# Attention and FFN in one kernel: the scores' second pass on half of TensorE's rows, a fifth PSUM bank, W_out sums on another engine, and a new order

## The chip, the cores and the metric

The kernel runs on one core of a Trainium2 chip. A core has TensorE (PE in the profile, with its weight loads listed as PEld), VectorE (DVE), ScalarE (ACT), GpSimd (POOL) and SyncE (SP, which issues the DMAs here). Each engine works through its own queue in the order in which it was filled, and waits on semaphores for the others. The metric is the device time of one execution in microseconds (us); what is compared is the median of several runs.

## The reference

Block-causal attention over 8 batches, 8 heads, 576 positions and a head size of 64, followed by a feed-forward block. All arithmetic is fp32.

```python
scores = q @ k.T / sqrt(64)                    # per batch and head, 576 x 576
scores = where(block_i >= block_j, scores, -1e9)   # blocks of 64 positions
attn = softmax(scores)
x = (attn @ v) -> (4608 tokens, 512)
h = x @ w_in                                   # 512 x 2048
g = h * sigmoid(h)
out = g @ w_out                                # 2048 x 512
```

## The kernel before

**fp32 by two halves.** TensorE's fast form for fp32 data ("fp32r" in the code) keeps fewer bits of each number, so most products are made of a rounded part ("hi") and what is left ("lo"). For the scores, a unit's tile `qk` holds the transposed q and k of one head twice, in partitions 0 to 63 and again in 64 to 127. `split_hi` (ScalarE) rounds it into `qh`. `split_k` (GpSimd) replaces the k part in partitions 64 to 127 with the remainder, so that a matmul with all 128 rows adds up k_hi and k_lo in one go. `split_q` (GpSimd) makes `ql`, the remainder of q. The scores are then two passes over the same keys: k times `qh`, and k times `ql`.

**Units.** A unit is one head of one batch (u0 to u63); it handles the 448 query positions from 128 on. (The first 128 positions are done ahead of that, by the objects a, b and c0 to c3.) The keys are cut into five groups of at most 128 (`SEG`): group 0 with 448 queries, group 1 with 448, group 2 with 320, group 3 with 192 and group 4 (64 keys) with 64. `scores` makes ten matmuls for a unit: pass one and pass two of key group 0, then of groups 2, 3, 1 and 4. Their results lie in three PSUM banks (`BANKS`): group 0 in the first, groups 2 and 3 in the second, groups 1 and 4 in the third. Units take the three banks in turn from four (`NS = 4`, S0 to S3). VectorE then takes maxima (`max`), subtracts them (`sub`), ScalarE takes the exponentials (`exp`), GpSimd and VectorE sum them, and for every second unit `pv` multiplies the exponentials of two units with v, in plain fp32, on two halves of TensorE's columns (tile `U`).

**The FFN.** The products x times w_in (`ffn1`, tokens `ffn` in the order; tile `h`) use the same hi and lo parts, three products of the four. One `ffn` token is half of a tile of h, six matmuls with 448 tokens each in the batches after the first positions; there are 320 of them. `keep` copies h out of PSUM and `save` writes it to DRAM. The second product (`prod`, at the end) is a Strassen-like scheme that needs sums of quarters of w_out and of g. The sums of w_out are made by the objects t0 to t7: `Turned.x` makes three sums, `hi` rounds, `lo` makes the remainder; `bits` of the objects o0 to o15 ahead of it rebuild w_out's numbers from the words in which they arrive, by way of the PSUM bank SC.

**What sets the order.** `ORDER` is a long string of tokens, worked through from left to right; each token calls one method and so appends its instructions to the engines' queues. `u20.scores` calls `Unit.scores` of unit 20; `ffn` calls the next half of h; `warm:10` issues ten small matmuls that no result uses. Nothing else moves instructions. Tiles and PSUM banks are handed out in that order too, and the waits between engines follow from it.

**The lines.** L702 is the matmul of the scores, L805 that of `pv`, L1031 that of the FFN's first product, L1108 that of the second. L834 is `warm`. L906, L934, L972 and L1003 are small matmuls for the first positions, on quarters (64 rows by 64 columns) or halves of TensorE. L683 is `split_k`, L687 `split_q`, L616 to L620 are the sums of w_out, L635 its remainders, and L541 the first step of `bits`.

Of the kernel before, what the change touches and what calls it, by code (L numbers as in the profile page):

```python
# [68 lines left out]
a.load b.load a.load_v w0.load b.load_v warm:10 a.scores w1.load w2.load a.max:0 a.sub:0 warm:3 b.scores c0.load a.max:1 a.sub:1  # L69
b.max:0 a.exp w3.load b.max:1 w4.load a.sum w0.rebias w0.sign w5.load b.sub:0 w6.load a.norm b.sub:1 w7.load w0.bits:0 b.exp  # L70
w0.bits:2 o1.load w1.rebias w1.sign warm:30 a.turn:0 b.sum w0.hi a.turn:1 a.back:0 w8.load w0.lo a.back:1 w1.bits:0 w2.rebias
warm:2 a.pv o0.load w1.bits:2 b.norm a.hi:0 c0.load_v a.hi:1 a.lo:0 w1.hi a.lo:1 w2.sign warm:7 b.turn:0 w3.rebias c3.load
c0.scores:0 b.back:0 b.turn:1 w5.rebias w1.lo w2.bits:0 w4.rebias ffn c0.max:0 b.back:1 w3.sign w2.bits:2 c0.exp:0 w9.load b.pv
w3.bits:0 c0.scores:1 w10.load all.mask b.hi:0 w3.bits:2 b.hi:1 ffn w2.hi c0.max:1 c3.load_v w3.hi w2.lo b.lo:0 c0.exp:1 b.lo:1
w4.bits:0 w3.lo ffn c0.sum w6.rebias c1.load w4.bits:1 w7.rebias c0.norm w4.bits:2 ffn keep w11.load w8.rebias w5.bits:0 w4.hi
save c0.turn:0 w5.bits:1 keep w4.lo c3.scores:0 w12.load c0.back:0 w5.bits:2 o1.rebias c0.turn:1 c3.max:0 w5.hi ffn save w6.bits:0
c0.back:1 w5.lo c3.exp:0 w6.bits:1 w13.load c0.pv w6.bits:2 c3.scores:1 c0.hi c1.load_v w7.bits:0 w6.hi ffn c0.lo w10.rebias
w14.load w6.lo c3.max:1 w9.rebias w7.bits:1 c3.exp:1 c1.scores:0 w7.bits:2 ffn c1.max:0 w15.load keep c3.sum c1.exp:0 save
w8.bits:0 c3.norm ffn w8.bits:1 w7.hi w8.bits:2 c1.scores:1 keep w7.lo w9.bits:0 c3.turn:0 w11.rebias save c1.max:1 w8.hi c2.load
ffn w9.bits:1 c3.back:0 w8.lo c1.exp:1 w9.bits:2 c3.turn:1 ffn w10.bits:0 c3.back:1 c1.sum w10.bits:1 w9.hi c1.norm c3.pv keep  # L80
w10.bits:2 w12.rebias ffn save w11.bits:0 w10.hi w9.lo w13.rebias w11.bits:1 c1.turn:0 o0.rebias w11.bits:2 ffn w10.lo c1.back:0
w12.bits:0 w11.hi w14.rebias c1.turn:1 w12.bits:1 w11.lo ffn c1.back:1 w12.bits:2 keep w13.bits:0 w15.rebias save c1.pv w12.hi
w13.bits:1 ffn w12.lo c1.hi c2.load_v w13.bits:2 c1.lo w13.hi c2.scores:0 w14.bits:0 keep w13.lo w14.bits:1 save ffn u0.load
c2.max:0 w14.bits:2 c2.exp:0 ffn w15.bits:0 w15.bits:1 w14.hi c2.scores:1 w15.bits:2 keep w14.lo ffn save c2.max:1 w15.hi u1.load
o0.bits:0 w15.lo all.staged c2.exp:1 ffn o0.bits:1 o0.bits:2 u0.split_hi ffn c2.sum o2.load o1.bits:0 c2.norm keep o1.bits:1
t0.hi:0 ffn save o1.bits:2 u0.split_q t0.hi:1 o3.load c2.turn:0 keep ffn u0.split_k c2.back:0 save c2.turn:1 ffn u2.load t0.x:0
c2.back:1 t0.x:1 c2.pv t0.hi:2 keep t0.x:2 u0.load_v ffn c2.hi save t0.lo:0 c3.hi u2.load_v c2.lo t0.hi:3 u3.load_v t0.lo:2 ffn
c3.lo u1.load_v t0.lo:3 u0.scores keep u0.max:0 t0.lo:1 save u0.max:1 ffn u1.split_hi u0.max:2 o2.rebias ffn u1.split_q u0.gather
o2.bits:0 o3.rebias u1.split_k u0.top ffn o2.bits:1 u0.spread u0.wide keep u3.load ffn u0.sub:0 u0.sub:1 save u0.exp:0 u1.scores
u0.sub:2 u0.exp:1 u0.exp:2 u1.max:0 ffn u1.max:1 u2.split_hi u0.add:0 u1.max:2 keep ffn u2.split_q u0.sums:0 u1.gather save  # L90
o2.bits:2 u0.add:1 u1.top ffn u1.spread o4.load o3.bits:0 u2.split_k u1.wide keep t1.hi:0 ffn u0.sums:1 save u1.sub:0 u4.load
t1.lo:0 u1.sub:1 u1.exp:0 u2.scores keep u1.sub:2 u1.exp:1 save u2.max:0 ffn u1.exp:2 u2.max:1 u3.split_hi u1.add:0 u2.max:2 u1.pv
u3.split_q u1.sums:0 u2.gather o3.bits:1 u2.top u3.split_k o3.bits:2 u2.spread ffn o5.load t1.hi:1 u2.wide u5.load u1.add:1
u2.sub:0 u2.sub:1 u3.scores t1.x:0 u2.exp:0 u4.load_v keep u3.max:0 u5.load_v u2.exp:1 save u1.sums:1 t1.x:1 ffn u4.split_hi
u3.max:1 t1.x:2 u3.max:2 t1.hi:2 ffn u4.split_q t1.hi:3 u2.sub:2 u3.gather u4.split_k ffn u1.sums_x u2.exp:2 u3.top u2.sums:0
u3.spread ffn u6.load u1.sums_g u2.add:0 u3.wide keep u3.sub:0 u2.add:1 u3.sub:1 save u4.scores u3.exp:0 keep u4.max:0 u1.sums_m
u3.exp:1 u2.sums:1 save ffn u5.split_hi u3.sub:2 u4.max:1 u5.split_q u3.exp:2 ffn u4.max:2 u3.add:0 ffn u1.inverse keep u4.gather
u1.mult save u3.add:1 u3.pv u4.top u3.sums:0 u4.spread u5.split_k u3.sums:1 u1.x_hi u4.wide u3.sums_x u4.sub:0 u7.load u1.x_lo
u3.sums_g u4.sub:1 u5.scores u4.exp:0 u6.load_v u4.sub:2 u3.sums_m u4.exp:1 u7.load_v u5.max:0 u4.exp:2 ffn u5.max:1 u6.split_hi
u4.add:0 u5.max:2 ffn keep u3.inverse u6.split_q u5.gather save ffn u5.top u3.mult u5.spread u4.add:1 u4.sums:0 u3.x_hi u5.wide  # L100
u6.split_k ffn keep u4.sums:1 save u5.sub:0 ffn u5.sub:1 u8.load u3.x_lo u5.exp:0 u5.sub:2 u5.exp:1 t1.lo:3 u6.scores u5.exp:2
u6.max:0 keep u5.add:0 u6.max:1 u5.pv save u7.split_hi u6.max:2 u5.add:1 u5.sums:0 u6.gather u7.split_q u5.sums:1 u6.top ffn
u5.sums_x u8.load_v u6.spread u7.split_k u9.load_v u5.sums_g u6.wide ffn u6.sub:0 u9.load u5.sums_m u6.sub:1 u6.exp:0 u7.scores
u6.sub:2 u6.exp:1 u6.exp:2 u7.max:0 t1.lo:1 u7.max:1 ffn keep u8.split_hi save u7.max:2 u6.add:0 ffn o5.rebias u5.inverse
u8.split_q u7.gather u5.mult ffn keep u7.top u6.add:1 u6.sums:0 u7.spread save u8.split_k ffn u5.x_hi u7.wide o4.rebias u6.sums:1
u7.sub:0 ffn u10.load u5.x_lo keep u7.sub:1 u7.exp:0 save u7.sub:2 u7.exp:1 t1.lo:2 u8.scores o4.bits:0 u7.exp:2 u8.max:0 u7.add:0
u7.pv u8.max:1 u9.split_hi u8.max:2 u7.add:1 u9.split_q u7.sums:0 u8.gather u7.sums:1 ffn u10.load_v u8.top u7.sums_x u9.split_k
u8.spread o4.bits:1 u11.load_v u7.sums_g u8.wide ffn u8.sub:0 keep u11.load u7.sums_m u8.sub:1 u8.exp:0 u9.scores save u8.sub:2
u8.exp:1 u9.max:0 u8.exp:2 ffn u9.max:1 u10.split_hi u8.add:0 u9.max:2 ffn u10.split_q keep u7.inverse u9.gather save u10.split_k
ffn u9.top u7.mult u9.spread u8.sums:0 u7.x_hi u9.wide ffn u12.load u7.x_lo keep u9.sub:0 u9.sub:1 save u9.exp:0 u8.add:1  # L110
u10.scores u9.sub:2 u9.exp:1 u10.max:0 u9.exp:2 u9.pv u10.max:1 u11.split_hi u10.max:2 u11.split_q u8.sums:1 u10.gather u9.sums:0
ffn u11.split_k u12.load_v u10.top o4.bits:2 u10.spread u13.load_v u10.wide t2.hi:0 ffn u13.load u9.add:0 keep u10.sub:0 u10.sub:1
u10.exp:0 save u9.add:1 u11.scores u10.sub:2 u10.exp:1 t2.lo:0 u11.max:0 u10.exp:2 ffn u9.sums:1 u12.split_hi u11.max:1 u10.add:0
ffn u11.max:2 keep u12.split_q save u9.sums_x u11.gather u10.sums:0 ffn u11.top u10.add:1 u9.sums_g o5.bits:0 u11.spread
u12.split_k ffn u10.sums:1 keep u11.wide u11.sub:0 save ffn u9.sums_m u14.load u11.sub:1 u11.exp:0 u12.scores u11.sub:2 u11.exp:1
u11.exp:2 u12.max:0 u12.max:1 ffn keep u11.add:0 u13.split_hi save u12.max:2 ffn u11.add:1 u9.inverse u12.gather u13.split_q ffn
# [1132 lines left out]
```

## Time and profile before

The columns of the last four rows are us of busy time of each engine in a stretch of the span.

| | |
|---|---|
| median of 3 runs | 999.03 us (998.24 to 1000.21) |
| the profiled execution | 999.48 us, of which the span of the program is 997.8 us |
| 0 to 76 us: first positions, weights | PE 71.53, DVE 53.85, ACT 55.14, POOL 47.28 |
| 76 to 560 us: the 64 units, with FFN between | PE 484.00, DVE 431.60, ACT 356.00, POOL 381.08 |
| 560 to 628 us: the rest of the first product; w_out is prepared | PE 68.00, DVE 28.70, ACT 38.92, POOL 43.03 |
| 628 to 998 us: the second product | PE 363.65, DVE 254.23, ACT 242.28, POOL 144.63 |

A matmul's end in the profile is modelled and matmuls overlap in it, so PE's busy time does not tell whether TensorE was at its peak. The distance from one matmul's start to the next tells it better: in the rows of the timeline the first column is the start, the second how long the row lasts.

### The profile page before, as it was taken

To read this page: it belongs to the slowest core of one execution; us is meant where nothing else is said; L and a number is where in the kernel's file an instruction comes from. 1 tells how busy PE (TensorE), PEld (TensorE's weight loads), DVE (VectorE), ACT (ScalarE), POOL (GpSimd) and SP (SyncE) were. 2 spreads that over 40 slices of the span, in tenths; PEclk is the share of its full clock that TensorE was granted. 3 is DMA by queue.
4 is the path that set the end of the run, shared out by engine and by line. 5 is a ranking of instruction groups with operands and counts; after the bars stand their busy time and mean duration, and the time that the engine had idled before them with its cause. 6 is when DMAs were issued, how large, how long until landed. Compare 5 with 4: busy or idle time off the path is not lost. (4 is left out here: it accounts for less than half of the span.)

```text
span 997.8 us, 20716 instructions
## 1 busy us (share of the span) xinstructions
PE 987.2 (99%) x6936; PEld 888.9 (89%) x6936; DVE 768.4 (77%) x1969; ACT 692.4 (69%) x1555; POOL 616.0 (62%) x722
## 2 busy tenths in 40 slices
...
GB/s 351 387 195 187 170 144 154 151 145 149 159 147 147 149 159 142 146 166 144 145 149 148 76 208 216 179 164 154 127 128 132 145 128 127 128 126 143 135 43 44
DMA packets 109803, 155.51 MB, mean 156 GB/s; under 512 B 18560, under 2 KB 83072, under 8 KB 109696
## 3 DMA queue, kind: packets, MB, share of 16 engines
...
## 5 line engine op out<-in xcount | busy, mean ns | idle before, releaser
L1031 PE MATMUL h<-x,wi 128*128 128x448 f32 (+2 forms) x1968 | 422.4, 370 | 0.3 <-POOL wi L563 0.3
L1031 PEld LDWEIGHTS h<-x,wi 128*128 128x128 f32 x1968 | 357.3, 188 | 37.4 <-issue 0.9
L642 DVE TRANSPOSE_TENSOR_REDUCE Mx<-S 64x4 f32<-64x128 f32 (+4 forms) x384 | 130.4, 399 | 18.1 <-PE S L702 17.1
L755 ACT ACTIVATE p<-T 128x512 f32<-128x512 f32 (+1 forms) x192 | 114.2, 613 | 21.0 <-DVE T L745 16.1
L1037 ACT COPY g<-h 128x448 f32<-128x448 f32 (+1 forms) x160 | 86.4, 540 | 50.9 <-PE h L1031 36.0
L1096 POOL TENSOR_TENSOR x<-raw,x 128x512 fp32r<-128x512 f32 (+1 forms) x58 | 58.8, 1016 | 78.2 <-ACT x L1092 73.9
L1059 ACT ACTIVATE raw<-raw 128x1024 f32<-128x1024 f32 x72 | 76.3, 1061 | 41.7 <-DMA raw<-gdb 36.4
L1096 POOL TENSOR_TENSOR wi<-raw,wi 128x512 fp32r<-128x512 f32 (+1 forms) x56 | 56.7, 1017 | 77.6 <-ACT wi L1092 67.5
L761 POOL TENSOR_TENSOR pa<-p 128x448 f32<-128x448 f32 x64 | 73.5, 1149 | 48.4 <-ACT p L755 41.2
L683 POOL TENSOR_TENSOR qh<-qk,qh 64x576 fp32r<-64x576 f32 x64 | 91.4, 1428 | 5.0
L702 PE MATMUL S<-qh 128*128 128x448 f32 (+3 forms) x320 | 92.8, 303 | 0.0
L687 POOL TENSOR_TENSOR ql<-qk,qh 128x448 fp32r<-128x448 f32 x64 | 73.6, 1149 | 24.0 <-ACT qh L677 17.0
L677 ACT CAST qh<-qk 128x1024 fp32r<-128x1024 f32 x64 | 67.1, 1048 | 28.8 <-PE S L702 15.1
L805 PE MATMUL U<-p,v 128*64 128x448 f32 (+3 forms) x640 | 86.5, 416 | 0.0
L702 PE MATMUL S<-ql,qh 128*128 128x448 f32 (+3 forms) x320 | 83.9, 306 | 0.0
L805 PEld LDWEIGHTS U<-p,v 128*64 128x64 f32 x640 | 43.0, 137 | 42.3 <-issue 31.0
L748 DVE TENSOR_TENSOR T<-S,MR 128x384 f32<-128x384 f32 (+2 forms) x192 | 73.3, 408 | 0.0
L702 PEld LDWEIGHTS S<-ql,qh 128*128 128x128 f32 (+1 forms) x320 | 57.0, 178 | 6.5
L702 PEld LDWEIGHTS S<-qh 128*128 128x128 f32 (+1 forms) x320 | 56.8, 178 | 3.7
L764 POOL TENSOR_TENSOR pa<-pa,p 128x320 f32<-128x320 f32 x64 | 55.9, 873 | 2.5
L1096 POOL TENSOR_TENSOR gc<-raw,gc 128x512 fp32r<-128x512 f32 (+1 forms) x30 | 30.4, 1017 | 41.4 <-ACT gc L1092 33.5
L727 ACT COPY m<-m 32x14 f32<-32x14 f32 x192 | 38.7, 202 | 20.1 <-DVE m L723 18.0
...
## 6 DMA issues: line engine op xcount, KB each, us to landing
qk<-in_qk_dram SPq DMA_DIRECT2D x128, 256.0 KB, 3.8
gdb<-g SPq DMA_DIRECT2D x128, 224.0 KB, 2.3
...
```

Source lines behind the costliest of these rows:

```text
L642: nc.vector.tensor_reduce(out=out, in_=in_, axis=AX.X, op=op, apply_transpose=True)
L683: nc.gpsimd.tensor_tensor(out=u.qh[r, c], in0=u.raw[r, c], in1=u.qh[r, c], op=ALU.subtract)
L687: nc.gpsimd.tensor_tensor(out=u.ql, in0=u.raw[:, :NQ], in1=u.qh[:, :NQ], op=ALU.subtract)
L702: nc.tensor.matmul(u.ps(c, w, m), u.kk[r, j * P : j * P + m], q[r, q0 : q0 + w], start=qq == 0 and not (ROWS and seg in (2, 4)), stop=qq = ...
L748: nc.vector.tensor_tensor(out=u.T[:, c + 64 : c + w], in0=u.ps(c + 64, w - 64), in1=u.mb[:, q0 + 64 : q0 + w], op=ALU.subtract)
L755: nc.scalar.activation(u.p[:, c:e], u.T[:, c:e], AF.Exp, scale=SCALE)
L761: nc.gpsimd.tensor_tensor(out=u.pa, in0=u.p[:, :NQ], in1=u.p[:, 960 : 960 + NQ], op=ALU.add)
L805: nc.tensor.matmul(U[64 * e : 64 * e + 64, q0 : q0 + w], u.vv[:, e, j], z.p[:, c : c + w], start=n == 0, stop=n == 4)
L1031: nc.tensor.matmul(o, wi[wt][:, c, w], x_of(g, c, xt), start=c + k == 0, stop=c == CT - 1 and k == 2)
L1037: nc.scalar.copy(g, hs.pop(z)[:, :n])
L1059: nc.scalar.activation(u.raw, u.raw, AF.Silu)
L1096: e.tensor_tensor(out=u.goal(1, k), in0=u.source(k), in1=u.goal(0, k), op=ALU.subtract)
```

## The change

- `ROWS = True`: the second pass (with `ql`) of key groups 0, 2 and 3 uses 64 rows of TensorE in place of 128. Group 0 uses partitions 0 to 63 and groups 2 and 3 use partitions 64 to 127. The product k_lo times q_lo is left out for these groups. Groups 1 and 4 keep all 128 rows.
- For that, the halves of k are laid otherwise (`LOWS`): keys 0 to 255 have their remainder in partitions 64 to 127 as before, keys 256 to 575 in partitions 0 to 63. `split_k` is two instructions in place of one.
- The passes come in another order (`PASSES`): first pass of groups 0, 2, 3; second pass of 0, 2, 3; then groups 1 and 4 as before.
- `NS = 5`: a unit's three banks are taken in turn from five; the bank SC is the fifth. `bits` for w_out works in its own tile instead of SC.
- `X_BY_VECTOR = (0,)` and `LO_BY_VECTOR = (1, 3)`: for t3 to t7 the first of the three sums and two of the four remainders are made by VectorE in place of GpSimd.
- A new `ORDER`, with the same tokens but for `warm` (63 small matmuls in place of 52).

```diff
-NS = 4
...
-LO_BY_VECTOR = ()
+LO_BY_VECTOR = (1, 3)
+X_BY_VECTOR = (0,)
+NS = 5
...
-ROWS = False
+ROWS = True
...
 if ROWS:
-    LOWS = [(64, 0, 128), (64, 384, 576), (0, 128, 384)]
-    PASSES = [(i, 0, (0, 128)) for i in range(5)] + [(4, 1, (0, 64)), (1, 1, (64, 128)), (0, 1, (0, 64)), (3, 1, (64, 128)), (2, 1, (0, 64))]
+    LOWS = [(64, 0, 256), (0, 256, 576)]
+    FULL, LOW, HIGH = (0, 128), (0, 64), (64, 128)
+    PASSES = [(0, 0, FULL), (1, 0, FULL), (2, 0, FULL), (0, 1, LOW), (1, 1, HIGH), (2, 1, HIGH), (3, 0, FULL), (3, 1, FULL), (4, 0, FULL), (4, 1, FULL)]
 else:
     LOWS = [(64, 0, 576)]
     PASSES = [(i, k, (0, 128)) for i in range(5) for k in range(2)]
...
             elif j == 0:
-                u.a = bank("C").bitcast(U32)
+                u.a = (bank("C") if u.kind == "in" or NS < 5 else u.w).bitcast(U32)
...
         def x(u, k):
 
             q, sub = u.w, ALU.subtract
+            e = nc.vector if u.d >= NTA and k in X_BY_VECTOR else nc.gpsimd
             if k == 0:
                 u.sums = sp.tile([P, 4, 256], F32, tag="xs", name="xs")
-                nc.gpsimd.tensor_tensor(out=u.sums[:, 0:2], in0=q[:, 1:4:2], in1=q[:, 0:2], op=sub)
+                e.tensor_tensor(out=u.sums[:, 0:2], in0=q[:, 1:4:2], in1=q[:, 0:2], op=sub)
...
         def lo(u, k):
             s, n = u.source(k)
-            e = nc.vector if k in LO_BY_VECTOR else nc.gpsimd
+            e = nc.vector if u.d >= NTA and k in LO_BY_VECTOR else nc.gpsimd
...
         def scores(u):
-            banks = [bank((3 * u.i + k) % NS) for k in range(3)]
+            banks = [bank((0, 1, 2, 3, "C")[(3 * u.i + k) % NS]) for k in range(3)]
...
-                nc.tensor.matmul(u.ps(c, w, m), u.kk[r, j * P : j * P + m], q[r, q0 : q0 + w], start=qq == 0 and not (ROWS and seg in (2, 4)), stop=qq == 1, skip_group_check=ROWS)
+                nc.tensor.matmul(u.ps(c, w, m), u.kk[r, j * P : j * P + m], q[r, q0 : q0 + w], start=qq == 0 and not (ROWS and seg == 2), stop=qq == 1 and not (ROWS and seg == 1), skip_group_check=ROWS)
```

(In `PASSES` the first number is a place in `SEG`: 0 is key group 0, 1 is group 2, 2 is group 3, 3 is group 1, 4 is group 4.)

**TensorE, the scores of unit 40.** A row is: line, instruction, output tile, inputs, and the output's shape (partitions by columns, so 64x64 is key group 4). `qh` alone on the right is pass one, `ql,qh` is pass two. Before, from the first score to key group 1:

```order
L702 MATMUL S_5337<-qh 128x448
L702 MATMUL S_5337<-ql,qh 128x448
L702 MATMUL S_5338<-qh 128x320
L702 MATMUL S_5338<-ql,qh 128x320
L702 MATMUL S_5338<-qh 128x192
L702 MATMUL S_5338<-ql,qh 128x192
L702 MATMUL S_5339<-qh 128x448
```

Now (three lines were added above, so L702 is L705):

```order
L705 MATMUL S_5436<-qh 128x448
L705 MATMUL S_5437<-qh 128x320
L705 MATMUL S_5437<-qh 128x192
L705 MATMUL S_5436<-ql,qh 128x448
L705 MATMUL S_5437<-ql,qh 128x320
L705 MATMUL S_5437<-ql,qh 128x192
L705 MATMUL S_5438<-qh 128x448
```

The three `ql,qh` rows now stand together, and these three are the ones on 64 rows; the rows ahead of and behind them use all 128.

**TensorE, the product with v that follows unit 40's scores (L805, now L808, for units 38 and 39).** Before:

```order
L702 MATMUL S_5339<-qh 64x64
L702 MATMUL S_5339<-ql,qh 64x64
L805 MATMUL U<-p,v 64x448 x4
L805 MATMUL U<-p,v 64x320 x2
L805 MATMUL U<-p,v 64x192 x2
L805 MATMUL U<-p,v 64x64 x2
L1031 MATMUL h<-x,wi_78 128x448 x2
```

Now:

```order
L705 MATMUL S_5438<-qh 64x64
L705 MATMUL S_5438<-ql,qh 64x64
L1034 MATMUL h<-x,wi_78 128x448 x2
L1034 MATMUL h<-x,wi_79 128x448
L1034 MATMUL h<-x,wi_78 128x448 x2
L1034 MATMUL h<-x,wi_79 128x448
L808 MATMUL U<-p,v 64x448 x4
L808 MATMUL U<-p,v 64x320 x2
```

One half of h (six matmuls) now stands between the scores and the product with v. Of the 32 such products, 25 stood right behind a unit's scores and 8 do now.

**GpSimd, in the middle of the units.** Before:

```order
L761 TENSOR_TENSOR pa<-p 128x448
L687 TENSOR_TENSOR ql<-qk,qh 128x448
L764 TENSOR_TENSOR pa<-pa,p 128x320
L683 TENSOR_TENSOR qh<-qk,qh 64x576
L817 TENSOR_TENSOR x<-xu,x 128x448
```

Now:

```order
L764 TENSOR_TENSOR pa<-p 128x448
L690 TENSOR_TENSOR ql<-qk,qh 128x448
L767 TENSOR_TENSOR pa<-pa,p 128x320
L686 TENSOR_TENSOR qh<-qk,qh 64x256
L686 TENSOR_TENSOR qh<-qk,qh 64x320
L820 TENSOR_TENSOR x<-xu,x 128x448
```

The remainder of k is two instructions of 256 and 320 columns in place of one of 576.

More of the change, by code (lines that the diff above doesn't have):

```diff
@@ L68 @@
 ORDER = """
[L69 to L116, printed above, removed]
@@ L384 @@
[L384 to L386 removed]
+a.load b.load_v b.load a.load_v w0.load warm:10 a.scores w1.load w2.load a.max:0 c0.load a.max:1 a.sub:0 a.sub:1 warm:10 b.scores
+w3.load a.exp a.sum w4.load w5.load w6.load b.max:0 a.norm w0.rebias b.max:1 w7.load b.sub:0 b.sub:1 w1.rebias w0.sign warm:19
@@ new lines @@
+c0.sum b.hi:1 c3.load_v all.mask b.lo:0 w4.hi b.lo:1 ffn c0.norm keep w5.rebias save w6.rebias c3.scores:0 w5.bits:0 w7.rebias
+w4.lo c0.turn:0 w5.bits:1 w12.load w8.rebias c3.max:0 ffn c0.back:0 w5.bits:2 c3.exp:0 w6.bits:0 w13.load c0.turn:1 ffn w6.bits:1
+c0.back:1 keep w6.bits:2 c0.pv w5.hi save w7.bits:0 w6.hi w14.load w5.lo c3.scores:1 c0.hi w7.bits:1 c1.load_v w9.rebias ffn c0.lo
+w6.lo w10.rebias c3.max:1 o1.rebias w7.bits:2 c1.scores:0 c3.exp:1 o1.bits:0 w15.load ffn w8.bits:0 c1.max:0 keep c3.sum c1.exp:0
@@ new lines @@
+save ffn w8.bits:1 c3.norm o1.bits:1 w8.bits:2 ffn w7.hi o1.bits:2 keep w7.lo w9.bits:0 w8.hi save c3.turn:0 w11.rebias o3.load
+w9.bits:1 c1.scores:1 w8.lo c3.back:0 ffn w9.bits:2 w12.rebias c2.load c1.max:1 w9.hi w10.bits:0 c1.exp:1 w9.lo c3.turn:1
+w10.bits:1 ffn w10.bits:2 c3.back:1 c1.sum ffn keep w11.bits:0 c1.norm w10.hi save w11.bits:1 o0.rebias c3.pv keep w11.bits:2
+w14.rebias w10.lo save o0.bits:0 c1.turn:0 w11.hi ffn w12.bits:0 c1.back:0 w11.lo o0.bits:1 w13.rebias w12.bits:1 c1.turn:1
@@ new lines @@
+w15.rebias ffn o0.bits:2 c1.back:1 w12.bits:2 t0.x:0 o2.load c1.pv w13.bits:0 w12.hi keep w12.lo w13.bits:1 ffn c1.hi save
+w13.bits:2 c2.load_v t0.x:1 c1.lo w13.hi ffn t0.x:2 w14.bits:0 w13.lo w14.bits:1 c2.scores:0 keep w14.bits:2 ffn save c2.max:0
+w14.hi u0.load w15.bits:0 c2.exp:0 w14.lo ffn w15.bits:1 w15.bits:2 c2.scores:1 keep ffn w15.hi save c2.max:1 u1.load w15.lo
+all.staged c2.exp:1 ffn u0.split_hi c2.sum ffn c2.norm keep t0.hi:0 ffn save t0.hi:1 t0.hi:2 u0.split_q t0.hi:3 c2.turn:0 keep ffn
@@ new lines @@
+u5.load_v u2.wide ffn keep o4.bits:1 u5.load u1.sums_m u2.sub:0 u3.scores u2.sub:2 save u2.exp:0 u2.sub:1 u2.exp:2 t1.lo:2 ffn
+u4.split_hi u3.max:0 u3.max:1 u2.add:0 u2.exp:1 ffn u3.max:2 keep u4.split_q save u2.sums:0 u3.gather ffn u1.inverse u2.add:1
+u3.top u1.mult u3.spread ffn u4.split_k u2.sums:1 keep u3.wide u1.x_hi save ffn o4.bits:2 u6.load u1.x_lo u3.sub:0 t2.hi:0
+u3.sub:2 u3.exp:0 u4.scores t2.lo:0 keep u3.sub:1 u3.exp:2 t1.lo:3 save ffn u4.max:0 u3.exp:1 u4.max:1 u5.split_hi u3.add:0
@@ new lines @@
+u27.max:1 u28.split_hi ffn u27.max:2 u26.add:1 keep u28.split_q u26.sums:0 save ffn u27.gather u26.sums:1 u27.top u25.inverse
+u28.split_k u27.spread ffn keep u27.wide u25.mult save ffn u30.load u27.sub:0 u25.x_hi u27.sub:2 u27.exp:0 u28.scores u25.x_lo
+keep u27.sub:1 u27.exp:2 save ffn u28.max:0 u27.exp:1 u27.add:0 u28.max:1 u29.split_hi u27.pv u28.max:2 u27.add:1 u27.sums:0
+u29.split_q u28.gather u27.sums:1 u28.top u27.sums_x u28.spread u29.split_k ffn u30.load_v u27.sums_g u28.wide u31.load_v
@@ new lines @@
+u34.add:0 u35.max:2 ffn u36.split_q u34.sums:0 u35.gather ffn u33.inverse keep u34.add:1 u35.top u33.mult save u35.spread ffn
+u36.split_k u34.sums:1 u33.x_hi u35.wide ffn keep u35.sub:0 u38.load u33.x_lo u35.sub:2 u35.exp:0 u36.scores u35.sub:1 save
+u35.exp:2 u36.max:0 u35.add:0 u35.exp:1 u35.pv u36.max:1 u37.split_hi u36.max:2 u35.add:1 u37.split_q u35.sums:0 u36.gather
+u35.sums:1 ffn u38.load_v u36.top u35.sums_x u39.load_v u37.split_k u36.spread ffn keep u36.wide u35.sums_g save u36.sub:0
```

566 lines of the change are left out of this document (294 added, 272 removed).

## The prediction

> **What bounds the kernel now.** I read the page first, then busy time by stage, then who waited for whom, and last the timeline of one unit.
>
> ```profile
> PE 987.2 (99%) x6936; PEld 888.9 (89%) x6936; DVE 768.4 (77%) x1969; ACT 692.4 (69%) x1555; POOL 616.0 (62%) x722
> 0.00:76.00 76.00, 71.53 (x832) 59.38 (x833) 53.85 (x89) 55.14 (x146) 47.28 (x50) 1.00 0.88 312
> 76.00:560.00 484.00, 484.00 (x2740) 406.16 (x2739) 431.60 (x1277) 356.00 (x890) 381.08 (x484) 1.00 0.52 150
> 560.00:628.00 68.00, 68.00 (x347) 61.68 (x346) 28.70 (x50) 38.92 (x75) 43.03 (x46) 1.00 0.59 190
> L702 PE MATMUL S<-qh x320: 192/309/469, 76.0 to 556.9; 128*128 128x448 f32 x64, 128*128 128x192 f32 x32, 128*64 128x64 f32 x32, 128*128 128x320 f32 x32
> ```
>
> In the stage rows the columns are PE, PEld, DVE, ACT and POOL. While the units run, PE is busy without a break, DVE 431.60 of 484 us (89%), POOL 79%, ACT 74%. The scores run from 76.0 to 556.9 us, so a unit takes 480.9 / 63 = 7.63 us. Busy time of PE is modelled, so I ask what PE waited for. These are all the waits of weight loads between 120 and 560 us (who waited, for whom: us in total, times, longest), and PE's matmuls have none:
>
> ```profile
> PEld U L805 <- issue: 28.5, 122, 0.3
> PEld U L805 <- DVE xu L809: 0.7, 2, 0.4
> PEld U L805 <- DVE dj L779: 0.3, 1, 0.3
> ```
>
> Only 1.0 us in 440 goes to another engine. The 28.5 us of "issue" stand at the product with v, and will matter below. So in this stage TensorE's own work sets the time, and a change of one unit's PE time counts 64 times. The timeline of one unit (start, how long the row lasts, what):
>
> ```profile
> 299.70 3.40 PE L1031 MATMUL h<-x,wi 128*128 128x448 f32 x16
> 302.94 0.36 PE L702 MATMUL S<-qh 128*128 128x448 f32 x1
> 303.15 0.37 PE L702 MATMUL S<-ql,qh 128*128 128x448 f32 x1
> 303.35 0.31 PE L702 MATMUL S<-qh 128*128 128x320 f32 x1
> 303.50 0.30 PE L702 MATMUL S<-ql,qh 128*128 128x320 f32 x1
> 303.64 0.25 PE L702 MATMUL S<-qh 128*128 128x192 f32 x1
> 303.73 0.27 PE L702 MATMUL S<-ql,qh 128*128 128x192 f32 x1
> 303.84 0.39 PE L702 MATMUL S<-qh 128*128 128x448 f32 x1
> 304.07 0.36 PE L702 MATMUL S<-ql,qh 128*128 128x448 f32 x1
> 304.27 0.19 PE L702 MATMUL S<-qh 128*64 128x64 f32 x1
> 304.30 0.22 PE L702 MATMUL S<-ql,qh 128*64 128x64 f32 x1
> 304.45 2.70 PE L805 MATMUL U<-p,v 128*64 128x448 f32 x20
> ```
>
> From start to start, 448 columns take 0.20 us ((302.94 - 299.70) / 16 = 0.2025), 320 take 0.15 and 192 take 0.09, or 0.11 where the weights for the next one are not in yet. The stretch that is rebuilt, from the first score to the second pass of key group 1, lasts 304.07 - 302.94 = 1.13 us.
>
> **The change part by part. The gain: matmuls side by side.** Two matmuls on different halves of the rows, with the same columns and different PSUM banks, do start together (S takes partitions 0 to 63, U 64 to 127):
>
> ```profile
> 4.46 0.36 PE L906 MATMUL S<-qk 64*64 64x64 f32 x1 [1.02 <-DMA qk<-in_qk_dram]
> 4.47 0.36 PE L906 MATMUL U<-qk 64*64 64x64 f32 x1
> ```
>
> The distance is 0.01 us. So group 0's second pass (448 columns, 0.20) can run beside those of groups 2 and 3 (0.15 + 0.11). If nothing else came of it, the stretch would be 0.20 + 0.15 + 0.11 (the three first passes) + 0.01 + 0.15 + 0.11 + 0.23 (group 1's first pass, as now) = 0.96 us. That is 0.17 less, 10.9 us over 64 units.
>
> **The price: going from 128 rows to 64 and back.** The kernel does this already in the first 70 us, and each time the start of the next matmul is late. First matmuls, then weight loads, around the cleanest case: plain fp32 on both sides, 64 columns on both sides, no wait, only the rows go from 64 to 128.
>
> ```profile
> 18.82 0.26 PE L934 MATMUL U<-p,v 64*64 64x64 f32 x2
> 18.88 0.22 PE L934 MATMUL U<-p,v 64*64 64x64 f32 x1
> 19.03 0.27 PE L834 MATMUL h<-zero 128*64 128x64 f32 x1
> 18.82 0.14 PEld L934 LDWEIGHTS U<-p,v 64*64 64x64 f32 x1
> 19.02 0.13 PEld L834 LDWEIGHTS h<-zero 128*64 128x64 f32 x1
> ```
>
> One such matmul of U follows the other by 0.06 us (18.82, 18.88); the first with 128 rows comes after 0.15. That is 0.09 us lost, and its weights are loaded only then (19.02), not ahead. It shows in that matmul's length, 0.27 against 0.22. The same from and to the FFN's matmuls:
>
> ```profile
> 39.55 0.39 PE L1031 MATMUL h<-x,wi 128*128 128x512 f32 x1
> 39.87 0.33 PE L972 MATMUL S<-qk 64*64 64x128 f32 x2
> 40.69 0.27 PE L972 MATMUL S<-qk 64*64 64x128 f32 x1
> 40.89 0.50 PE L1031 MATMUL h<-x,wi 128*128 128x512 f32 x1
> L972 PE MATMUL S<-qk x128: 268/269/320, 21.3 to 62.5; 64*64 64x128 f32 x128
> L1031 PE MATMUL h<-x,wi 128*128 128x512 f32 x336 | 83.8, 399 | 0.0
> ```
>
> Going in: 0.32 where 512 columns take 0.2025 x 512 / 448 = 0.23, so 0.09 lost, and the first matmul lasts 0.320 against 0.269 us, 0.05 for weights of 64 columns. Coming out: 0.20 where 128 columns at twice the 0.06 take 0.12, so 0.08 to 0.09, and the first one lasts 0.50 against 0.399, 0.10 for weights of 128 columns. The new scores have weights of 128 columns on both sides. I take 0.09 for each switch and 0.10 for the weights behind it. The stretch then is 0.20 + 0.15 + (0.09 + 0.09) + 0.01 + (0.15 + 0.10) + (0.09 + 0.09) + (0.20 + 0.10) = 1.27 us. (In the last term the 0.20 replaces the 0.23, whose 0.03 is the same wait for weights.) Against 1.13 this is 0.14 more, **9.0 us** over 64 units.
>
> One thing speaks against this price. No row has the switch in the fast fp32 form: all matmuls on 64 rows are plain fp32, and the form alone can cost as much (304.30 to 304.45 above: from S to U, both 128*64, 0.15 where S's own step is 0.03). Within the fast form a change of columns, 128*128 to 128*64 at 304.27, costs nothing: 0.20 ahead of it as for any 448 columns, 0.03 after. So the price lies between nothing and the 0.31 that 1.27 - 0.96 makes. I take the full one, since the row at 19.03 has no change of form and is the only one with rows alone.
>
> The Trainium skill, page "TensorEngine Tiling (Array Packing)", section Key Properties, says that changing the tiling mode, not just the tile, drains TensorE. The row at 19.03 agrees; the step at 304.27, a change of mode by its shape, shows no drain. By the rule as written the sum is the one above; by the step at 304.27 it would be the gain alone.
>
> **The products with v behind the FFN.** 17 of 32 no longer follow a unit's scores. The scores then hand over to h directly:
>
> ```profile
> 312.26 0.22 PE L702 MATMUL S<-ql,qh 128*64 128x64 f32 x1
> 312.31 0.45 PE L1031 MATMUL h<-x,wi 128*128 128x448 f32 x1
> L1031 PE MATMUL h<-x,wi 128*128 128x448 f32 x1536 | 326.0, 369 | 0.0
> ```
>
> Its first matmul lasts 0.45 against 0.369, since the short key group 4 does not cover its weight load: 0.08 us, 17 times, **1.4 us**. The entry into U costs about as much from h as from S.
>
> **What costs nothing, and its cover.** GpSimd's and VectorE's rows for the moved work:
>
> ```profile
> L683 POOL TENSOR_TENSOR qh<-qk,qh 64x576 fp32r<-64x576 f32 x64 | 91.4, 1428 | 5.0
> L616 POOL TENSOR_TENSOR xs<-wraw 128x512 f32<-128x512 f32 x8 | 10.3, 1294 | 5.0 <-DVE wraw L551 4.8
> L620 POOL TENSOR_TENSOR xs<-wraw,xs 128x256 f32<-128x256 f32 x8 | 5.9, 739 | 0.5
> L1096 DVE TENSOR_TENSOR x<-h,x 128x512 fp32r<-128x512 f32 x30 | 19.8, 685 | 6.7 <-ACT x L1092 6.5
> ```
>
> 256 more columns cost GpSimd 0.555 us, so an instruction has a fixed 0.18; the second `split_k` adds that per unit. GpSimd's free 1.6 us of each 7.63 cover it; without cover it would be 11.5 us. The W_out sums: three instructions of t3 to t7, 1.294 us each on GpSimd, about 0.685 on VectorE, which is free for 39 of the 68 us to 628. PE is fully busy there with the FFN, so it is worth nothing; the 5 halves of h that stand earlier now take 5 x 6 x 0.2025 = 6.1 us of cover from this stage, less than the 9.1 us (15 x 0.61) that the sums get shorter. If the cover fails, up to 6 us. The fifth bank can bring at most the 1.0 us that PE waits for others: nothing. The new start: PE is free for 4.5 of the first 76 us; 11 more small matmuls and another order can move that either way by 3 us. I take nothing.
>
> **Sum.** 9.0 + 1.4 = 10.4 us on the profiled execution's own 999.48 us (span 997.8): 1009.9. The median lies 0.45 lower, so **1009.4 us**.
>
> **The rivals.** *Rows cost nothing in the fast form* (faster). Then the stretch is 0.96 us and the sum -10.9 + 1.4 = -9.5: 989.5 us. For it: the free step at 304.27. Against it: 19.03. It decides as soon as the two switches cost less than 0.15 us together (0.17 less the 1.4 / 64). VectorE would not stop it: 6.80 us of work in a unit of 7.48 is 91%.
> *Half the price*: only the late start (0.18, weights loaded ahead) or only the weights (0.20). The stretch is then about 1.12 or 1.09, the sum -0.6 + 1.4 or -2.6 + 1.4: 998 to 1000 us. Against it: in every switch above both come together.
> *The change doesn't do what it says*: the 64-row matmuls in the fast form follow one another. That adds 0.19 us to the forecast's stretch, 12.2 us: 1021.6. Against it: 4.46 and 4.47, though in plain fp32 and with 64 columns.
>
> **How the numbers follow.** The full price 0.58, rows for nothing 0.27, half the price 0.09, one after another 0.06. The likeliest one's own range is 1005 to 1014 (start and cover). The range over all is 987 to 1014; it leaves out the last rival and what strays. A measurement can tell 0.2%, 2.0 us, from no change. Faster: 0.27 and a little of the half price, 0.28. The same: 0.10. Slower: 0.62.
>
> **What would show it.** Per unit, the start of the first `ql,qh` row 0.18 behind the 192-column row before it, the second one 0.01 later, group 1's first pass 0.18 behind the last; new waits of weight loads put down to "issue" at S; a unit of 7.79 us. I am wrong if those steps are 0.09 to 0.11, if the two tiles do not start together, or if PE waits for other engines between 76 and 628 us.

## The result, and the profile after

The changed kernel takes **1010.29 us** (median of 4 runs, 1009.70 to 1011.45) against 999.39 us for the kernel before (4 runs, 998.24 to 1000.21). The ratio is 1.0111, with a 95% interval from 1.0094 to 1.0129. It is slower by 10.9 us; the forecast was 1009.4 us. Two single runs of the experiments below (1710.63 us with the rows last, 1356.37 us with group 1 too in the new order) had a granted clock of 0.75 in place of 1.00 and are in no median.

First the same stages of the changed kernel (start and end of the stretch, its length, then busy us of PE, PEld, DVE, ACT and POOL with their instructions, the granted clock, the DMA share and GB/s):

```profile
0.00:76.00 76.00, 68.64 (x819) 57.63 (x820) 53.31 (x87) 53.78 (x144) 46.69 (x49) 1.00 0.84 302
76.00:560.00 484.00, 483.83 (x2706) 388.45 (x2705) 419.10 (x1227) 344.72 (x863) 384.07 (x531) 1.00 0.53 150
560.00:628.00 68.00, 67.48 (x347) 58.44 (x346) 46.71 (x104) 38.37 (x86) 32.05 (x43) 1.00 0.46 147
```

Then the first passes of the scores that lie in S (count; shortest, median and longest ns; first and last start; shapes):

```profile
L705 PE MATMUL S<-qh x257: 191/309/477, 80.9 to 575.1; 128*128 128x448 f32 x39, 128*128 128x192 f32 x39, 128*64 128x64 f32 x39, 128*128 128x320 f32 x12
```

TensorE is still busy nearly all the time while the units run (483.83 of 484 us), the clock is still 1.00, and VectorE and ScalarE do a little less in the same 484 us. So next to nothing new waits; the same work lasts longer. The units start at 80.9 us in place of 76.0, and one takes (575.1 - 80.9) / 63 = 7.84 us in place of 7.63. Three more halves of h, 18 matmuls, now stand between the first score and the last; at 0.206 us each they make 0.06 us of this. (Units now use five banks in turn, so a fifth of the results lies in SC, in a group of rows of its own.)

The waits of weight loads between 120 and 560 us, all of them:

```profile
PEld U L808 <- issue: 32.2, 132, 0.3
```

One unit in the timeline of matmuls (start, how long the row lasts, what):

```profile
303.82 0.36 PE L705 MATMUL SC<-qh 128*128 128x448 f32 x1
304.03 0.40 PE L705 MATMUL S<-qh 128*128 128x320 f32 x2
304.35 0.46 PE L705 MATMUL SC<-ql,qh 64*128 64x448 f32 x1
304.36 0.50 PE L705 MATMUL S<-ql,qh 64*128 64x320 f32 x2
304.79 0.47 PE L705 MATMUL S<-qh 128*128 128x448 f32 x1
305.10 0.37 PE L705 MATMUL S<-ql,qh 128*128 128x448 f32 x1
305.30 0.19 PE L705 MATMUL S<-qh 128*64 128x64 f32 x1
305.33 0.22 PE L705 MATMUL S<-ql,qh 128*64 128x64 f32 x1
305.39 0.45 PE L1034 MATMUL h<-x,wi 128*128 128x448 f32 x1
```

And the timeline of weight loads in the same stretch:

```profile
304.35 0.18 PEld L705 LDWEIGHTS SC<-ql,qh 64*128 64x128 f32 x1
...
304.79 0.19 PEld L705 LDWEIGHTS S<-qh 128*128 128x128 f32 x1
304.89 0.19 PEld L705 LDWEIGHTS S<-ql,qh 128*128 128x128 f32 x1
```

The two `ql,qh` rows on 64 rows start 0.01 us apart (304.35, 304.36): the tiles do work side by side. But at both switches the weights arrive with the matmul and not ahead of it (304.35 on both lists, 304.79 on both), and the matmul behind it comes 0.31 us later (304.79 to 305.10), where 448 columns otherwise take 0.20 (305.10 to 305.30).

Over all 64 units I took the mean distance from each matmul's start to the next one's, from the start times of both traces. "Switch" is a step between 128 rows and 64.

| from, to | before | after |
|---|---|---|
| 448 columns on 128 rows, next | 0.21 | 0.21 |
| 320 columns on 128 rows, next | 0.15 | 0.15 |
| 192 columns on 128 rows, next | 0.09 to 0.11 | 0.18 (switch) |
| 448 columns on 64 rows, 320 on the other 64 | - | 0.003 |
| 320 columns on 64 rows, 192 on the same | - | 0.25 |
| 192 columns on 64 rows, group 1's first pass | - | 0.18 (switch) |
| group 1's first pass, its second | 0.23 | 0.31 |
| first score to group 1's second pass | 1.141 | 1.283 |

The last row is 0.142 us more, 9.1 us over 64 units.

### The profile page after: what moved, and what is told of

It reads as the page before. It is cut to its first block, busy times and chain, and to the rows that moved or that the text cites. A ratio compares the mean times of both kernels' runs of the same rounds, so it can differ in the third digit from the quotient of the medians.

```text
span 1009.7 us, 20872 instructions
## 1 busy us (share of the span) xinstructions
PE 996.3 (99%) x6958; PEld 878.3 (87%) x6958; DVE 783.8 (78%) x1984; ACT 690.4 (68%) x1555; POOL 614.6 (61%) x771
## 5 line engine op out<-in xcount | busy, mean ns | idle before, releaser
L1034 PE MATMUL h<-x,wi 128*128 128x448 f32 (+2 forms) x1968 | 426.9, 371 | 1.3 <-ACT g L1040 1.3
L645 DVE TRANSPOSE_TENSOR_REDUCE Mx<-S 64x4 f32<-64x128 f32 (+4 forms) x308 | 107.0, 401 | 24.7 <-PE S L705 16.8
L686 POOL TENSOR_TENSOR qh<-qk,qh 64x256 fp32r<-64x256 f32 (+1 forms) x128 | 103.8, 811 | 9.8
L808 PE MATMUL U<-p,v 128*64 128x448 f32 (+3 forms) x640 | 86.5, 416 | 0.0
L808 PEld LDWEIGHTS U<-p,v 128*64 128x64 f32 x640 | 43.1, 136 | 46.8 <-issue 37.2
L705 PE MATMUL S<-qh 128*128 128x448 f32 (+1 forms) x257 | 67.6, 318 | 0.2 <-POOL qh L686 0.2
L751 DVE TENSOR_TENSOR T<-S,MR 128x128 f32<-128x128 f32 (+2 forms) x154 | 58.8, 406 | 0.0
L705 PE MATMUL S<-ql,qh 64*128 64x448 f32 (+2 forms) x257 | 55.2, 341 | 0.0
L705 PEld LDWEIGHTS S<-qh 128*128 128x128 f32 x257 | 45.1, 177 | 11.5 <-POOL qh L686 0.6
L649 DVE STREAM_TRANSPOSE MR<-m 128x448 f32<-128x448 f32 x64 | 40.1, 626 | 13.9 <-ACT m L730 13.5
L654 ACT COPY mj<-mj 32x14 f32<-32x14 f32 x192 | 38.5, 201 | 16.6 <-DVE mj L719 14.1
```

The lines of the kernel that those rows point to most:

```text
L645: nc.vector.tensor_reduce(out=out, in_=in_, axis=AX.X, op=op, apply_transpose=True)
L686: nc.gpsimd.tensor_tensor(out=u.qh[r, c], in0=u.raw[r, c], in1=u.qh[r, c], op=ALU.subtract)
L705: nc.tensor.matmul(u.ps(c, w, m), u.kk[r, j * P : j * P + m], q[r, q0 : q0 + w], start=qq == 0 and not (ROWS and seg == 2), stop=qq == 1 a ...
L808: nc.tensor.matmul(U[64 * e : 64 * e + 64, q0 : q0 + w], u.vv[:, e, j], z.p[:, c : c + w], start=n == 0, stop=n == 4)
L1034: nc.tensor.matmul(o, wi[wt][:, c, w], x_of(g, c, xt), start=c + k == 0, stop=c == CT - 1 and k == 2)
```

## The experiments

Each was timed against the kernel before on the same chip (its median was 999.4 to 999.7 us there). Lines shown as removed are those of the kernel named.

**The rows alone, and all but the rows.** The changed kernel with the three second passes back on 128 rows (order of the passes, banks, sums and the new order kept):

```diff
-    LOWS = [(64, 0, 256), (0, 256, 576)]
+    LOWS = [(64, 0, 576)]
...
-(0, 1, LOW), (1, 1, HIGH), (2, 1, HIGH)
+(0, 1, FULL), (1, 1, FULL), (2, 1, FULL)
```

> The change with one part undone: the second pass of key groups 0, 2 and 3 uses all 128 rows again (and k's remainders lie in partitions 64 to 127 for all keys, by one instruction); the order of the passes, the order of the program, the five banks and the W_out sums stay as changed. Theory A (the two switches between 128 and 64 rows cost more than side by side saves): the stretch from a unit's first score to the second pass of key group 1 goes from 1.28 us to 0.20 + 0.15 + 0.11 + 0.205 + 0.147 + 0.114 + 0.225 = 1.15 us, 64 times 0.13 is 8.3 us, so 1002.0 us. Theory B (the time comes from the rest: products with v behind the FFN, the new start, the banks, the new order): 1010 us, no change.

The kernel before with `ROWS`, `LOWS`, `PASSES` and the flags of the matmul taken from the change, and nothing else:

```diff
-ROWS = False
+ROWS = True
...
-    LOWS = [(64, 0, 128), (64, 384, 576), (0, 128, 384)]
+    LOWS = [(64, 0, 256), (0, 256, 576)]
+    FULL, LOW, HIGH = (0, 128), (0, 64), (64, 128)
```

> The kernel before with one part of the change: the passes on 64 rows, their order and the halves of k; the order of the program, four banks and the W_out sums as before. The product k_lo times q_lo is left out for key groups 0, 2 and 3, as in the change. Theory A: each unit's stretch goes from 1.13 to 1.28 us, 64 times 0.155 is 9.9 us, so 999.4 + 9.9 = 1009.3 us. Theory B: 999.4 us, and less if side by side is a gain.

Measured: 1000.93 us without the rows (10 runs; ratio 1.0010, 0.9999 to 1.0021) and 1007.27 us with the rows alone (4 runs; 1.0068, 1.0051 to 1.0085). So the rows cost 1010.29 - 1000.93 = 9.4 us on the one side and 1007.27 - 999.55 = 7.7 on the other (2 less than expected), and all the rest together costs about 1.4, which is just short of being told from nothing. The part from a unit's first score to the next work that isn't a score, where that is h, takes 1.425 us on 128 rows and 1.572 in the changed kernel: 0.147 x 64 = 9.4 us, the whole difference between the two. (With the rows alone the scores' distances add up to 9.2 us more than before as well; in the second product they add up to 1.4 less.) One unit of the kernel without the rows in the timeline, in the new order of passes:

```profile
306.97 0.59 PE L705 MATMUL S<-qh 128*128 128x448 f32 x3
307.40 0.63 PE L705 MATMUL S<-ql,qh 128*128 128x448 f32 x3
307.86 0.39 PE L705 MATMUL SC<-qh 128*128 128x448 f32 x1
308.09 0.36 PE L705 MATMUL SC<-ql,qh 128*128 128x448 f32 x1
```

Six passes take 0.89 us here (306.97 to 307.86), 0.90 in the old order (302.94 to 303.84) and 0.97 in the changed kernel (303.82 to 304.79); and the step behind them is 0.23 in place of 0.31. The order of the passes as such changes nothing.

**Do the tiles work side by side at all?** All three 64-row passes on partitions 0 to 63, so that none can run beside another. This is the changed kernel; the switches are as many as there.

```diff
-    LOWS = [(64, 0, 256), (0, 256, 576)]
+    LOWS = [(64, 0, 576)]
...
-(0, 1, LOW), (1, 1, HIGH), (2, 1, HIGH)
+(0, 1, LOW), (1, 1, LOW), (2, 1, LOW)
```

> The change, but the three second passes on 64 rows all lie on the same half (partitions 0 to 63; the remainders of k in partitions 64 to 127 for all keys), so that there are as many switches and nothing is side by side. Theory A: group 0's second pass no longer runs beside the others, the step behind it goes from 0.003 to 0.20 us; 64 times 0.195 is 12.5 us, so 1022.8 us. If the change had got nothing from side by side: 1010.3 us.

Measured: 1024.26 us (4 runs; ratio 1.0237, 1.0215 to 1.0259), 14.0 more than the changed kernel, where 0.19 us of each unit (below) are 12.2; what is left is less than the interval of the ratio. One unit in its timeline, from group 3's first pass on:

```profile
301.75 0.25 PE L705 MATMUL S<-qh 128*128 128x192 f32 x1
301.93 0.47 PE L705 MATMUL S<-ql,qh 64*128 64x448 f32 x1
302.24 0.39 PE L705 MATMUL S<-ql,qh 64*128 64x320 f32 x2
302.56 0.47 PE L705 MATMUL S<-qh 128*128 128x448 f32 x1
302.87 0.36 PE L705 MATMUL S<-ql,qh 128*128 128x448 f32 x1
```

The switches are the same (301.75 to 301.93, 0.18; 302.56 to 302.87, 0.31). What is new is the step from 301.93 to 302.24: 0.31 where the changed kernel has 0.003. From the first 64-row matmul to group 1 it takes 0.63 us (302.56 - 301.93) against 0.44 (304.79 - 304.35). So working side by side is real and is worth 0.19 us per unit; the loss lies at the switches.

**Twice as many switches.** Group 1's first pass is put between the 64-row passes, in the changed kernel: four switches per unit, the same matmuls.

```diff
-(0, 1, LOW), (1, 1, HIGH), (2, 1, HIGH), (3, 0, FULL), (3, 1, FULL)
+(0, 1, LOW), (3, 0, FULL), (1, 1, HIGH), (2, 1, HIGH), (3, 1, FULL)
```

> The change with group 1's first pass (128 rows) put between the second passes of group 0 and of groups 2 and 3, so that a unit has four switches of rows and nothing side by side. Theory A, a switch costs 0.09 us late start and 0.10 us for weights that are loaded only then: steps 0.18, 0.39, 0.39, 0.25, 0.18, 0.30 from the 192-column first pass to key group 4, 0.56 us more a unit, 36 us, so 1046 us; of this 12.5 us are the lost side by side and 24 us the two more switches. If a switch is free and the change's time comes from elsewhere: 1010 to 1023 us.

Measured: 1047.10 us (2 runs; ratio 1.0467, 1.0439 to 1.0495). One unit in its timeline, from the first 64-row pass on:

```profile
302.49 0.46 PE L705 MATMUL S<-ql,qh 64*128 64x448 f32 x1
302.88 0.47 PE L705 MATMUL S<-qh 128*128 128x448 f32 x1
303.28 0.50 PE L705 MATMUL SC<-ql,qh 64*128 64x320 f32 x2
303.71 0.47 PE L705 MATMUL S<-ql,qh 128*128 128x448 f32 x1
```

With a switch on both sides a matmul of 448 columns takes 0.39 to 0.40 us (302.49, 302.88, 303.28): 0.20 of its own, 0.10 for its weights, 0.09 for the next late start, as the terms of the prediction say. Part of the 36.8 us over the changed kernel is that the pair is split as well, 0.19 x 64 = 12.2 us by the run before; the other 24.6 are 0.38 us per unit for two more switches, 0.19 each.

**Is it the rows, or any change of shape?** The kernel before with the rows, and group 4's second pass on 64 rows too, so that its tile goes from 64 rows by 128 columns to 64 by 64.

```diff
-(3, 0, FULL), (3, 1, FULL), (4, 0, FULL), (4, 1, FULL)]
+(3, 0, FULL), (4, 0, FULL), (0, 1, LOW), (1, 1, HIGH), (2, 1, HIGH), (4, 1, HIGH), (3, 1, FULL)]
```

(The three 64-row passes are taken out of their old place.)

> The kernel before with the change's 64-row passes, and group 4's second pass (64 keys, so 64 columns) on 64 rows too, right behind that of group 3: a step from 64 rows by 128 columns to 64 by 64. Beside what the change leaves out, k_lo times q_lo is left out for group 4 as well. Theory A, only a change of rows costs: that step starts 0.11 us behind the 192-column row as any other, and the time is that of the rows alone, 1007 within 2. Theory B, each change of the tile's shape on 64 rows costs: the step is 0.18 to 0.20 us, and the time 1012 to 1014.

Measured: 1012.05 us (4 runs; ratio 1.0120, 1.0103 to 1.0137). One unit in its timeline, from group 3's second pass on:

```profile
302.65 0.68 PE L703 MATMUL S<-ql,qh 64*128 64x192 f32 x3
302.74 0.59 PE L703 MATMUL S<-ql,qh 64*64 64x64 f32 x2
302.85 0.47 PE L703 MATMUL S<-ql,qh 128*128 128x448 f32 x1
303.16 0.37 PE L1032 MATMUL h<-x,wi 128*128 128x448 f32 x1
```

(The number behind x in the first two rows takes in the later ones; the starts are what counts.) The 64*64 matmul starts 0.09 us behind the 192-column one (302.65, 302.74), as 192 columns take anywhere: a change of columns on 64 rows is free. The next one, back to 128 rows, comes 0.11 later (302.74, 302.85) where 64 columns otherwise take 0.03, and the one behind that 0.31 later. Theory A holds for the step, but its time doesn't: 1012 is what B said. What else is new is a wait: group 1's first pass now stands ahead of the 64-row passes, so its bank is asked for 0.44 us behind the first score, not 0.97 as with the rows alone, and the scores' weight loads and matmuls wait, which they do not in the run with the rows alone (waits between 80 and 580 us):

```profile
PEld S L703 <- issue: 16.4, 79, 0.7
PE S L703 <- DVE T L740: 1.4, 5, 0.5
```

From the first score to the next work, the 64 units add up to 5.7 us more than if each took the median of its kind (0.5 with the rows alone), which covers the 4.8 us between the two runs.

**Can a switch be hidden?** The product with v is plain fp32, and the step from the scores to it costs 0.15 us in place of 0.03 before the change too. So the 64-row passes were put last in a unit, where one of the switches falls together with that step in 25 units. The kernel before with the rows, four banks:

```diff
-(0, 1, LOW), (1, 1, HIGH), (2, 1, HIGH), (3, 0, FULL), (3, 1, FULL), (4, 0, FULL), (4, 1, FULL)]
+(3, 0, FULL), (3, 1, FULL), (4, 0, FULL), (4, 1, FULL), (0, 1, LOW), (1, 1, HIGH), (2, 1, HIGH)]
```

> The kernel before with the change's 64-row passes, order of instructions between units and banks as before; only, the three 64-row passes stand last in a unit's scores (first passes of groups 0, 2, 3, both of group 1, both of group 4, then the three on 64 rows). So one switch per unit stands behind a matmul of 64 columns, and the other falls together with the step from the scores to the product with v (25 units), which costs 0.12 us by its change of form anyway, or to h (39 units). Theory A, a switch is hidden where the next step is a change of form as well: by the measured steps the part from the second pass of group 0 to the first product with v takes as long as before or 0.04 us less in 25 units, and 0.07 more in the 39 that go on to h: +1.8 us, 1001.4 us in all. Theory B, the two switches cost the same wherever they stand: 1007.3 us, as with the rows in the middle.

Measured: 1022.00 us (3 runs; ratio 1.0233, 1.0206 to 1.0260), more than either theory. The scores' waits in the whole run:

```profile
PEld S L703 <- issue: 14.2, 39, 0.9
PE S L703 <- DVE T L740: 6.2, 26, 0.7
```

One of them in the timeline:

```profile
314.76 0.44 PE L703 MATMUL S<-qh 128*128 128x448 f32 x1 [0.20 <-DVE T L740]
```

Group 1's first pass now comes fourth in a unit, 0.44 us behind the first score and not 0.97 as with the rows alone (0.91 before), and waits for VectorE (L740 is the subtraction of the maxima, the last to read such a bank for an earlier unit). Where nothing waited, the part from the first score to the next work took 1.478 us in front of the product with v (before: 1.505) and 1.472 in front of h (before: 1.406 at the least). That is theory A for the steps, but the time went to a wait that I had not put into it. The same with the fifth bank, and with `bits` in its own tile as in the change:

```diff
-NS = 4
+NS = 5
...
-            banks = [bank((3 * u.i + k) % NS) for k in range(3)]
+            banks = [bank((0, 1, 2, 3, "C")[(3 * u.i + k) % NS]) for k in range(3)]
```

> As the run with the three 64-row passes last in a unit's scores, with the fifth PSUM bank in addition (old order, W_out sums on GpSimd as before). Theory A, that run lost its time to the bank of key groups 1 and 4, which the new order of passes asks for 0.5 us earlier, while VectorE still works on it: with five banks the waits of the scores for VectorE go, the part from the first score to the next work of another kind takes 1.47 us in front of h and 1.48 in front of the products with v in nearly all units, and the time is 1001 to 1005 us (1.7 us for the rows, up to 3.6 for what the fifth bank costs with the old order). Theory B, the passes at the end are late for VectorE for another reason (the results of groups 0, 2 and 3 are ready only at the end): the waits stay and the time is 1015 or more.

Measured: 1008.03 us (4 runs; ratio 1.0088, 1.0073 to 1.0103). The waits of matmuls of the scores between 76 and 560 us, all of them:

```profile
PE S L705 <- POOL qh L686: 0.3, 1, 0.3
PE S L705 <- DVE T L748: 0.2, 1, 0.2
```

The waits are gone, and with them 14 us. The median of the part in question is 1.476 us in front of the product with v and 1.478 in front of h, as expected. The total lies between the theories: 3 us over the upper end of A. By the distances from start to start, matmuls of the scores take 3.3 us more than before and those of h 6.9. Of these 6.9, 2.2 are two gaps at 68 and 72 us, which belong to the next experiment; 0.9 are a gap at 114 us, which the rows-last run with four banks has too; and these waits for ScalarE's copy of h behind the units are part of the others (between 560 and 640 us):

```profile
PEld h L1034 <- ACT g L1040: 2.1, 3, 1.1
PE h L1034 <- ACT g L1040: 0.9, 2, 0.7
```

**The edits that were taken to cost nothing.** The changed kernel with the old order and 128 rows, which leaves the fifth bank and the W_out sums on VectorE:

```diff
-ROWS = True
+ROWS = False
...
 ORDER = """ (that of the kernel before) """
```

> The changed kernel with the old order of instructions and all second passes on 128 rows, so that only the fifth bank and the W_out sums on VectorE are left of the change. Theory A, both are covered: 999.5 us, within 1. Theory B, the 1.4 us by which the changed kernel on 128 rows lay above the kernel before come from them: 1001. If A holds, what is left of the 1.4 belongs to the new order.

Measured: 1002.97 us (10 runs; ratio 1.0031, 1.0021 to 1.0041): neither within 1 us nor 1.4, but 3.6 more than before. Most of it stands at the start: the first score comes at 78.5 us in place of 76.0, and among PE's waits are these two (L865, L862 before, is a matmul that transposes a tile of the first positions, L868 ScalarE's copy of such a tile out of PSUM).

```profile
PE S L865 <- POOL p L858: 2.5, 1, 2.5
PE S L865 <- ACT MR L868: 1.7, 1, 1.7
```

The second is in all three traces that have five banks with the old order (1.7 us in each) and in none with four. The first is in traces with four as well, the rows alone among them (2.6 us), whose units started at 76.4; so I don't count it. The order of the changed kernel doesn't have this wait of 1.7 us, but starts its units at 80 to 81 us. Two of those three runs, rows last with five banks and the one with group 1 too (below), make the W_out sums on GpSimd as before; so this wait comes with the bank and `bits` in its own tile, and not with the sums. No run has the sums without the bank, so what they cost by themselves stays open.

**More work for the same two switches.** Group 1's second pass on 64 rows as well: two passes of 448 columns on one half, 320 and 192 on the other. First with the old order (the run with rows last and five banks, changed in its passes and in the matmul's start flag, which follows them):

```diff
-(3, 0, FULL), (3, 1, FULL), (4, 0, FULL), (4, 1, FULL), (0, 1, LOW), (1, 1, HIGH), (2, 1, HIGH)]
+(3, 0, FULL), (4, 0, FULL), (4, 1, FULL), (0, 1, LOW), (1, 1, HIGH), (3, 1, LOW), (2, 1, HIGH)]
```

> As the run before, with key group 1's second pass on 64 rows as well, behind group 2's: two passes of 448 columns on partitions 0 to 63 beside those of 320 and 192 on the others. k_lo times q_lo is left out for group 1 too. Side by side the second passes then take 0.40 us in place of 0.66: a gain of 0.26 per unit in place of 0.17, for the same two switches. Theory A: the part from the first score to the next work takes 1.39 to 1.41 us, that is 0.02 less in front of h and 0.10 less in front of the products with v than before the change; 3 to 5 us under the run with three passes at the end. Theory B, the tiles wait for each other within a half (weights of the second 448 columns are loaded only when the first are through, and cost 0.10 more): no gain against that run.

Then the same passes in the changed kernel:

> The changed kernel, whole (new order, five banks, W_out sums on VectorE), with the second passes of groups 0, 2, 1 and 3 on 64 rows at the end of a unit's scores, as in the run before. Theory A: 0.02 us less per unit in front of h (56 units) and 0.10 in front of the products with v (8) than the changed kernel on 128 rows, 1000.9 - 2 = 999 us. Theory B: a switch at the end in front of h costs as much as in the middle, or VectorE, which gets a unit's results later, makes the scores wait: 1005 us or more.

Measured: 1003.42 us (4 runs; ratio 1.0040, 1.0025 to 1.0055) and 1002.86 us (6 runs; 1.0038, 1.0023 to 1.0052). With the old order that is 4.6 us under the run with three passes at the end, inside the 3 to 5 of theory A. With the new order it is 7.4 us under the changed kernel, but 2 over the same kernel on 128 rows, where theory A wanted 2 less; nor does it reach the 1005 of theory B. One unit of the run with the old order in the timeline:

```profile
307.71 0.66 PE L705 MATMUL S<-ql,qh 64*128 64x448 f32 x4
308.01 0.36 PE L705 MATMUL S<-ql,qh 64*128 64x448 f32 x1
308.30 0.60 PE L808 MATMUL U<-p,v 128*64 128x448 f32 x2
```

The second 448-column matmul of a half starts 0.30 us behind the first (307.71, 308.01): 0.20 and 0.10 for weights. That wait is the mechanism of theory B, although the time came out as A said. All four passes take 0.59 us (308.30 - 307.71). From the first score to the next work it is 1.43 to 1.44 us, where theory A wanted 1.39 to 1.41: 0.07 less than before in front of the product with v, but 0.02 more in front of h. The expected gain of 0.26 per unit is then about as large as the price, and no version here is faster than the kernel before.

## Why the prediction was right

**What bounds the kernel.** Held. TensorE was busy for 483.83 of 484 us while the units ran, and a unit's PE time counted 64 times: the step distances alone give 9.1 us, and two kernels that differ in the rows alone differ by 9.4 (the other such pair by 7.7, with 9.2 in the scores and 1.4 less in the second product).

**The gain: matmuls side by side.** Held, by more than was taken. 0.003 us between the two tiles, where 0.01 was taken. On one half only, the same passes need 0.19 us more per unit; the rival that they follow one another priced just this at 0.19.

**The price: going from 128 rows to 64 and back.** Held in its size and its two parts. Forecast: the stretch from 1.13 to 1.27 us, +0.14, 9.0 us; measured: 1.141 to 1.283, +0.142, 9.1 us. The late start is 0.18 - 0.09 = 0.09 us each time; the matmul behind the switch waits 0.10 more for its weights. In the kernel with four switches each further one costs 0.19. (One sum was off, without consequence: by the prediction's own terms the stretch with only the late starts, half the price, is 0.96 + 2 x 0.07 = 1.10 us, not 1.12.) That plain fp32 rows at 19.03 and 39.87 gave the price for the fast form was the doubtful step of the prediction, and it was the right row. The free step at 304.27 that spoke against it is no exception: it changes columns only, which the run with group 4 on 64 rows shows free on 64 rows too (0.09 us from 302.65 to 302.74). The Trainium skill's sentence in "TensorEngine Tiling (Array Packing)", section Key Properties, that a change of tiling mode drains TensorE agrees with these traces where the rows change (0.09 us late), and not where only the columns do (0.09 us behind 192 columns, as without a change).

**Products with v behind the FFN.** Forecast 1.4 us. The first matmul of h behind a unit's scores is followed by the next after 0.288 us instead of 0.206, now 56 times and not 39: 17 x 0.082 = 1.4 us. The entry into U from h is 0.10 us late, from S about as much (0.15 in place of 0.055 to h). So the size held.

**What costs nothing.** Only the sum held. `split_k` is covered: GpSimd's rows for it grew by 103.8 - 91.4 = 12.4 us (0.19 per unit) and the scores waited for `split_k` once, for 0.6 us, before the stretch from 120 us on that is shown above. GpSimd's row:

```profile
L686 POOL TENSOR_TENSOR qh<-qk,qh 64x256 fp32r<-64x256 f32 (+1 forms) x128 | 103.8, 811 | 9.8
```

The new start was taken as nothing, give or take 3. The first score came 4.9 us later: by the distances, 1.8 of it are h, of which two halves more now stand ahead of it, 3.1 are the 11 more `warm` matmuls, and the rest cancels. Behind the units h waited for ScalarE in two gaps, 1.6 us beyond its own steps, and the distances of the second product add up to 2.7 us less, for a reason that no run isolates. Together the changed kernel on 128 rows lay 1.4 us above the kernel before, which is the term for the products with v and leaves nothing. But "nothing" was made of effects against each other, so that its sum held was luck; and the fifth bank isn't free by itself: with the old order it and the sums cost 3.6 us, and the wait of 1.7 us at the start comes with the bank.

**What would show it.** Three signs came as written: 0.18 us ahead of the first `ql,qh` row, its neighbour at once, 0.18 ahead of group 1. Two did not. The new waits of weight loads at S are not in the list of waits: 0.09 us each is less than this view lists (in the kernel with four switches it lists such rows). And a unit took 7.84 us, not 7.79: the prediction left out the three halves of h that moved in between the units, 0.06 us a unit. The sign of a miss, that PE waits for other engines before 628 us, came in small: between 560 and 660 us the weight loads and matmuls of h waited for ScalarE's copy of h, none of which the kernel before has there (before 628 us it is 1.3 us of the weight loads and 0.5 of the matmuls).

```profile
PE h L1034 <- ACT g L1040: 1.3, 2, 0.8
PEld h L1034 <- ACT g L1040: 2.4, 3, 1.2
```
